# Reordering the start and the end of a fused convolution and maxout kernel: grouped transposes, one more column group with four taps on TensorE, relus ahead of copies, and a free bank and a merged store at the end

## The chip, the cores and the metric

The kernel runs on one core of a Trainium2 chip. A core has five engines with a queue of instructions each: TensorE (PE in the profile; its weight loads are shown apart as PEld), VectorE (DVE), ScalarE (ACT), GpSimd (POOL) and SyncE (SP, which here only issues DMAs). An engine works through its own queue in order; semaphores tie the queues together. The metric is the device time of one execution in microseconds (us). The kernel before takes 424.26 us, the median of 13 runs that lie between 422.1 and 426.3.

## The reference: what is computed

A dynamic convolution is followed by a maxout block. `x` is 8 x 4160 x 192; there are 8 heads of 24 channels, and every row and head has its own 7 weights.

```
w   = softmax(weight_gen, over the 7 taps)            # per row and head
y   = sum over k of w[.., k] * x_padded[row + k]       # causal: 6 zero rows ahead of each batch item
h1  = y @ w1 ; h2 = y @ w2                             # 33280 x 192 @ 192 x 1024
out = max(h1, h2) @ w_out                              # 33280 x 1024 @ 1024 x 192, float32
```

The kernel uses max(h1, h2) = h1 + relu(h2 - h1). So it computes relu(y @ (w2 - w1)) @ w_out + y @ (w1 @ w_out): one wide product in place of two, and a small one with the constant 192 x 192 matrix w1 @ w_out.

## The kernel before, in words

**Columns, batches, units, tiles, groups.** Partition p holds the rows 260p to 260p + 259. A *column* is one row of each partition: 128 rows. The 260 columns are taken in 17 *batches* of 16 (the last has 4). A batch is cut into *units*: four of 4 columns in batches 0 and 1, two of 8 columns afterwards, one of 4 at the end. A unit has as many *tiles* as columns; a tile is a [128 x 1024] block of hidden values in PSUM, which one or two of the eight 128-wide pieces of d_ff fill for all columns of the unit. Tiles are processed in *groups* (`GROUPS`, line 70): eight groups of two, then groups of three; the last group, with tile 259, has a single one. While a group's hidden tiles are made, the results of earlier columns (`OUTS`, line 366) are made too, two or four columns at a time. Eight columns are left when the groups are through; `rest_of_results` (line 426) makes them in three parts of 4, 2 and 2.

**The stages.** For each batch ACT takes exp of the weights (`exp_sum`, L127), DVE sums them over the taps (`red`, L132), ACT takes the log of the sum (`ln`, L135), DVE subtracts it (`shift`, L140), and ACT takes exp again, to bf16 (`weights`, L148). DVE multiplies seven shifted views of `x` by these (`mul`, L157, into `m_t`). The seven taps are then added and the result is transposed, in one of three ways:

- units 8 and up: DVE adds all (`adds`, L172, L177, L179, into `y_t`), a DMA issued on SP transposes (`transpose`, L188), and POOL waits for it with a small copy before it starts the next loads (L194);
- units 4 to 7: DVE makes the first add only (`adds(.., True)`, L172: taps 3 to 5 onto 0 to 2). TensorE multiplies the four taps left by the identity and accumulates them in PSUM, which transposes and adds at once (`sum_transpose`, L215), and ACT copies the sum out (L220);
- units 0 to 3: the same with all seven taps on TensorE.

`hid_tile` (L247) makes a hidden tile from the transposed `yt`, `relu` (L257, on ACT) moves it to `rd_t` in bf16. `out_first` (L299 and L287) and `out_second` (L287) accumulate results in a bank `op_ps`; half of the contributions use partitions 0 to 63 and half 64 to 127, and the second half waits, by an empty instruction on ACT (`relay`, L320), until the first is through. `evac` (L343) copies a result to `o_t`, and stores go out when a unit is complete (L353). The last two columns go apart (L333): one is copied on ACT and stored from ACT's queue, the other is copied on DVE and stored from SP's.

**Order.** The schedule is manual: each engine's instructions stand in the order in which the functions are called. The start (from line 450 on) is written out call by call. `early` (line 630) says what is put between the halves of groups 3 to 7, and `extra` (line 638) hangs the DVE, ACT and DMA work of later batches on tile numbers. Ahead of the work proper, TensorE multiplies the identity 115 times (`keep_warm`).

**PSUM.** In the start two pools of two buffers each are used: `h` for hidden tiles and `o` for everything else, in turn (column sums, the transposed w1 `tp`, the product `pw`, results). From group 8 on there are `ab` (2048 wide, the first two tiles of a group), `c` (1024, its last tile) and `r` (1024, the results), with one buffer each. A new tile in a pool waits for the last reader of the buffer that it takes over.

**w1 @ w_out.** `w1_transposed` (line 536) transposes the eight 128-wide pieces of w1 on TensorE: for each piece a part of 128 rows (`E`) and one of 64 (`T`), L542. Two ACT copies bring them to `w1t` (L548). `w10_product` (line 582) multiplies (L587), and five ACT copies (L595) write `w10`, which `out_first` needs.

Of the kernel before, what the change touches and what calls it, by code (L numbers as in the profile page):

```python
# [17 lines left out]
def _sub(base: bass.AP, off: int, dims):  # L18
    ap = [list(base.ap[0])] + [[int(s), int(c)] for s, c in dims]
    return dataclasses.replace(base, offset=base.offset + off, ap=ap)  # L20
# [3 lines left out]
def kernel(  # L24
# [9 lines left out]
    nc = tc.nc  # L34
# [90 lines left out]
    def exp_sum(b):  # L125
        e_ts[b] = pe_.tile([P, BATCHES[b][1] * WGC], FP32, name="e_t", tag="e")
        nc.scalar.activation(out=e_ts[b], in_=wg_ts[b], func=AF.Exp)  # L127

    def red(b):
        TH = BATCHES[b][1] * H  # L130
        s_ts[b] = psm.tile([P, TH], FP32, name="sum_t", tag="sum")
        nc.vector.reduce_sum(out=s_ts[b], in_=_sub(e_ts.pop(b), 0, [[K, TH], [1, K]]), axis=AX.X)  # L132

    def ln(b):
        nc.scalar.activation(out=s_ts[b], in_=s_ts[b], func=AF.Ln)  # L135
# [7 lines left out]
    def weights(b, o):  # L143

        N = dict(pieces(b))[o] * H
        if b not in en_ts:
            en_ts[b] = pen.tile([P, 16 * WGC * 2], BF16, name="en_t", tag="en")
        nc.scalar.activation(  # L148
            out=_sub(en_ts[b], o * WGC * 2, [[2 * N, K], [2, N], [1, 2]]),
            in_=_sub(wg_ts[b], o * WGC, [[1, K], [K, N], [0, 2]]), func=AF.Exp,  # L150
        )


    def mul(b, o):

        n = dict(pieces(b))[o]
        nc.vector.tensor_tensor(  # L157
            out=m_t[:, K * o * D:K * (o + n) * D],
            in0=_sub(xb_ts[b], o * D, [[D, K], [1, n * D]]),
            in1=_sub(en_ts[b], o * WGC * 2, [[2, K * n * H], [0, G // 2], [1, 2]]),  # L160
            op=ALU.mult,
        )
# [40 lines left out]
    def half(j):  # L203
        return slice(64 * j, 64 * j + 64)

    def sum_transpose(u, taps=range(K)):

        b, o, n = UNITS[u]
        nb = n // 2 * 3
        yps = ps["r" if "r" in ps else "o"].tile([P, 1024], FP32, name="yps", tag="op")  # L210
        for k in range(nb):
            for t in taps:
                for j in range(2):
                    at = (K * o + t * n + k // 3 + j * n // 2) * D + k % 3 * 64
                    nc.tensor.matmul(  # L215
                        yps[half(j), k * P:(k + 1) * P], lhsT=m_t[:, at:at + 64],
                        rhs=ident, start=(t == taps[0]), stop=(t == taps[-1]), skip_group_check=True,
                    )
        yt = pyt.tile([P, 8 // 2 * 3 * P], BF16, name="yt", tag="yt")
        nc.scalar.copy(out=yt[:, 0:nb * P], in_=yps[:, 0:nb * P])  # L220
        yt_ts[u] = yt
# [46 lines left out]
    def place(p):  # L268

        u, i, _ = column(2 * p)  # L270
        b, o, n = UNITS[u]
        return BATCHES[b][0] + o + i, n // 2
# [36 lines left out]
    def out_second(now, go):  # L309

        for c in now[::2]:
            for f in range(FCH):
                for j in range(2):
                    mm = out_hidden(c + 1 - j, f, j)
                    if c == now[0] and f == 0:
                        tc.add_manual_dep(mm.ins, go.ins.name, SYNC, reason="bank of the other half")
# [8 lines left out]
    def evac(p, n):  # L325

        tile_, at = op_at[p]
        o = o_t[0]
        if p == NT // 2 - 1:

            for j, copy, eng in ((0, nc.scalar.copy, nc.scalar), (1, nc.vector.tensor_copy, nc.sync)):
                c = place(p)[0] + 2 * j
                copy(out=o[:, c % 24 * D:(c % 24 + 1) * D], in_=tile_[:, at + j * 512:at + j * 512 + D])  # L333
                eng.dma_start(
                    out=bass.AP(tensor=out.tensor, offset=c * D, ap=[[CPP * D, P], [1, D]]),
                    in_=o[:, c % 24 * D:(c % 24 + 1) * D],
                )
            return
        runs = [[q for q in range(p, p + n) if column(2 * q)[0] == u]
                for u in range(column(2 * p)[0], column(2 * (p + n - 1))[0] + 1)]  # L340
        for qs in runs:
            c, h = place(qs[0])
            nc.scalar.copy(out=_sub(o, c % 24 * D, [[D, len(qs)], [h * D, 2], [1, D]]),  # L343
                           in_=_sub(tile_, at + (qs[0] - p) * D, [[D, len(qs)], [512, 2], [1, D]]))
        stores = []
        for q in range(p, p + n):
            u, i, _ = column(2 * q)
            if u < NU - 1 and i == UNITS[u][2] // 2 - 1:
                stores.append((place(q)[0] - i, 2 * (i + 1)))
            if u == NU - 1:  # L350
                stores.extend((place(q)[0] + 2 * j, 1) for j in range(2))
        for c, w in stores:
            nc.scalar.dma_start(  # L353
                out=bass.AP(tensor=out.tensor, offset=c * D, ap=[[CPP * D, P], [1, w * D]]),
                in_=o_t[0][:, c % 24 * D:(c % 24 + w) * D],
            )


# [32 lines left out]
    def out_room(now, tag=None):  # L391
        tag = tag or ("r" if "r" in ps else "o")
        w, name = {"ab": (2048, "ab"), "c": (1024, "c")}.get(tag, (1024, "op"))
        tile_ = ps[tag].tile([P, w], FP32, name="op_ps", tag=name)
        for c in now:
            op_at[c // 2] = tile_, (c - now[0]) // 2 * D

    def hidden(g, now=(), between=lambda: None, beside=lambda: None):


        t0, n = GROUPS[g]
        rd = room(g)
        for t in range(t0, t0 + n - 1):
            hid_tile(t)
        if now:
            out_room(now)
            last = out_first(now)
        if len(now) > 2:
            relu(rd, t0, n - 1)
        else:  # L410
            for t in range(t0, t0 + n - 1):
                relu(rd, t, 1)
        if now:
            go = relay(last)
        hid_tile(t0 + n - 1)
        if len(now) > 2:
            beside()
        relu(rd, t0 + n - 1, 1)
        between()
        if now:  # L420
            out_second(now, go)
            evac(now[0] // 2, len(now) // 2)
        if len(now) <= 2:
            beside()
# [25 lines left out]
    with tc.tile_pool(name="pstage", bufs=1) as pstage:  # L450
# [85 lines left out]
        def w1_transposed():  # L536

            tp = ps["o"].tile([P, 1024], FP32, name="tp", tag="op")[:, :].bitcast(BF16)
            for fi in range(FCH):
                o = fi // 4 * 1024 + fi % 4 * D  # L540
                for at, kind, nr in ((0, "E", P), (P, "T", 64)):
                    nc.tensor.matmul(  # L542
                        tp[:, o + at:o + at + nr],
                        lhsT=w1[kind][0:nr, fi * P:(fi + 1) * P],
                        rhs=ident[0:nr, 0:nr], is_transpose=True, skip_group_check=True,
                    )
            for h in range(2):
                nc.scalar.copy(out=w1t[:, 4 * h * D:4 * (h + 1) * D],  # L548
                               in_=tp[:, h * 1024:h * 1024 + 4 * D])

        warm = ps["h"].tile([P, 1024], FP32, name="warm", tag="hd")

# [15 lines left out]
        nc.scalar.copy(out=w1["T"], in_=ws["T", 0])  # L568
        w_diff(1, nc.vector.tensor_copy)
        mul(0, 8)  # L570
        sum_transpose(1)
        exp_sum(1)
        red(1)
# [1 line left out]
        ln(1)  # L575
        shift(1)
        mul(0, 12)
        w1_transposed()
        weights(1, 0)
        weights(1, 4)  # L580

        def w10_product():

# [13 lines left out]


        hidden(2)
        mul(1, 0)  # L600
        adds(1, 0, True)
        exp_sum(2)
        sum_transpose(2)
        load_x(2, 0, 16)
        load_wg(4, nc.gpsimd)
        red(2)
        mul(1, 4)
        adds(1, 4, True)
        hidden(3)
        w10_product()  # L610
        sum_transpose(3)
        weights(1, 8)
        weights(1, 12)
        ln(2)

    pout = ctx.enter_context(tc.tile_pool(name="pout", bufs=1))
    o_t.append(pout.tile([P, 24 * D], FP32, name="o_t", tag="o"))
# [2 lines left out]
    def rest_of_1():  # L620
        mul(1, 8)
        shift(2)
        adds(1, 8, True)
        mul(1, 12)
        red(3)
        adds(1, 12, True)


    none = lambda: None
    early = {  # L630
        3: (none, lambda: (exp_sum(3), rest_of_1())),
        4: (lambda: sum_transpose(4, (0, 1, 2, K - 1)), lambda: weights(2, 0)),
        5: (lambda: sum_transpose(5, (0, 1, 2, K - 1)), none),
        6: (lambda: (weights(2, 8), ln(3), sum_transpose(6, (0, 1, 2, K - 1))), lambda: load_x(3, 0, 8)),
        7: (lambda: sum_transpose(7, (0, 1, 2, K - 1)), none),
    }

    def extra(t):
# [29 lines left out]
    out_room(OUTS[3])  # L668
    go = relay(out_first(OUTS[3]))
    out_second(OUTS[3], go)  # L670
    evac(OUTS[3][0] // 2, len(OUTS[3]) // 2)
    early[3][1]()
    for g in range(4, len(GROUPS)):
# [40 lines left out]
```

## Time and profile before

| what | value |
|---|---|
| median of 13 runs | 424.26 us (422.1 to 426.3) |
| the profiled execution | 425.85 us, of which the span of the profile is 424.0 |
| TensorE clock granted, mean | 0.997 of full speed |
| ACT relus, L257, 128x1024 and 128x2048 | 206 instructions, 234.6 us |
| TensorE results, L287 | 4160 matmuls, 210.7 us |
| TensorE hidden tiles, L247 | 1584 matmuls, 187.4 us |
| DVE products, L157 | 37 instructions, 187.5 us |
| TensorE column sums, L215 | 528 matmuls, 16.5 us |
| instruction queue | 58 packets, 0.95 MB |

A timeline row gives the start in us from the start of the span, the time it covers in us, the engine, the line, the operation, what is written and read, the shapes, the number of instructions, and in square brackets the idle time before it with what ended it. "issue" there stands for nothing that the profile shows. Matmuls are pipelined and their ends are modelled, so the busy time of PE is no measure of its peak. The chain that ended last is followed back from the last instruction, at each step to what released it or to the instruction ahead of it on its engine.

### The profile page before, as it was taken

The page shows a single profiled execution, that of the slowest core. Times are in us where ns is not written, and L with a number is a line of the kernel's source. Part 1 is how long each engine was busy: PE and PEld are TensorE (multiplying, and loading weights), DVE is VectorE, ACT ScalarE, POOL GpSimd, SP SyncE. Part 2 cuts the span into 40 slices and gives each one's busy share as a digit, 9 for nine tenths or more (in the row PEclk, how much of TensorE's full clock was granted, in tenths as well). Part 3 has the DMA queues.
Part 4 walks back from the last instruction along what each step waited for, and adds up shares of the span by engine and source line. Part 5 has one row for each costly group of instructions (what it writes and reads, how often), then busy time and mean ns, then how long its engine had stood idle before and what let it go on. Part 6 is the DMA issues. An engine that isn't in the chain of part 4 may idle for free.

```text
span 424.0 us, 15949 instructions
## 1 busy us (share of the span) xinstructions
PE 406.7 (96%) x7405; PEld 329.3 (78%) x7405; DVE 377.1 (89%) x176; ACT 360.2 (85%) x416; POOL 69.9 (16%) x102
## 2 busy tenths in 40 slices
PE   7988999999999999999999999999999999999984
PEld 7867899877778777877777777877777777777784
DVE  5989998998999999999999999999999999996000
ACT  5795979999998989898989999898999899787851
POOL 1510102221112221222111212201311121210000
PEclk9999999999999999999999999999999999999998
DMA  8975436577687677965867677687796586556213
GB/s 249 255 160 147 112 77 157 99 161 125 170 193 154 183 174 100 237 166 125 233 112 176 169 177 191 146 147 197 98 251 165 89 211 116 117 157 129 80 77 114
DMA packets 60259, 65.70 MB, mean 155 GB/s; under 512 B 47617, under 2 KB 48513, under 8 KB 60192
## 3 DMA queue, kind: packets, MB, share of 16 engines
q0 software_dynamic: 8128, 24.11, 28.4%
q1 hardware_dynamic: 46448, 15.10, 21.7%
q10 hardware_dynamic: 5616, 25.46, 15.5%
q8 instruction: 58, 0.95, 0.9%
q14 instruction: 9, 0.07, 0.1%
HBM read 35.96 MB, written 25.56 MB: 145 GB/s over the span
## 4 chain that ended last, share of the span: by engine, by line
DVE 57%; PE 31%; ACT 7%; issue 4%; ACTq 1%; POOL 0%; DVEq 0%; POOLq 0%
DVE m_t L157 28%; DVE m_t L172 12%; PE op_ps L287 11%; DVE m_t L177 9%; PE hd L247 8%; ACT rd_t L257 4%; PE yps L215 4%; PE hdp L247 3%; DVE y_t L179 3%; DVE wg_t L140 3%; DVE sum_t L132 2%; PE warm L556 2%; PE op_ps L299 2%; ACT o_t L343 1%; ACTq L353 1%
## 5 line engine op out<-in xcount | busy, mean ns | idle before, releaser
L257 ACT ACTIVATE rd_t<-hd 128x1024 bf16<-128x1024 f32 (+1 forms) x206 | 234.6, 1183 | 31.4 <-PE hd L247 31.0
L287 PE MATMUL op_ps<-wo,rd_t 64*128 64x192 bf16 x4160 | 210.7, 243 | 1.9 <-issue 1.8
L287 PEld LDWEIGHTS <-rd_t 64*128 64x128 bf16 x4160 | 180.2, 94 | 18.2 <-issue 2.1
L247 PE MATMUL hd<-yt,wd 64*128 64x512 bf16 (+1 forms) x1584 | 187.4, 360 | 0.9 <-ACT rd_t L257 0.9
L157 DVE TENSOR_TENSOR m_t<-xb_t,en_t 128x10752 bf16<-128x10752 bf16 (+1 forms) x37 | 187.5, 5070 | 0.5 <-ACT rd_t L257 0.3
L247 PEld LDWEIGHTS <-wd 64*128 64x128 bf16 x1776 | 93.1, 94 | 43.4 <-issue 3.6
L194 POOL CAST gate<-yt 128x1 f32<-128x1 bf16 x29 | 34.0, 1172 | 285.9 <-DMA yt<-y_t 285.9
L172 DVE TENSOR_TENSOR m_t<-m_t 128x4608 bf16<-128x4608 bf16 (+1 forms) x33 | 78.2, 2368 | 0.1
L343 ACT COPY o_t<-op_ps 128x384 f32<-128x384 f32 (+1 forms) x99 | 56.9, 586 | 12.5 <-PE op_ps L287 12.4
L299 PE MATMUL op_ps<-w,yt 64*128 64x192 bf16 x780 | 55.4, 243 | 4.4 <-ACT o_t L343 4.4
L299 PEld LDWEIGHTS <-yt 64*128 64x128 bf16 x780 | 38.7, 94 | 21.4 <-issue 6.6
L177 DVE TENSOR_TENSOR m_t<-m_t 128x3072 bf16<-128x3072 bf16 (+1 forms) x29 | 50.2, 1730 | 1.0
L148 ACT ACTIVATE en_t<-wg_t 128x896 bf16<-128x896 f32 (+1 forms) x37 | 34.1, 935 | 1.9 <-ACT o_t L343 1.2
L333 DVE COPY o_t<-op_ps 128x192 f32<-128x192 f32 x1 | 0.4, 358 | 31.4 <-ACT o_t L333 31.4
L179 DVE TENSOR_TENSOR y_t<-m_t 128x1536 bf16<-128x1536 bf16 (+1 forms) x29 | 27.4, 944 | 1.0
L132 DVE TENSOR_REDUCE sum_t<-e_t 128x128 f32<-128x896 f32 (+1 forms) x17 | 17.7, 1038 | 5.3 <-ACT e_t L127 5.3
L115 POOL DMA_DIRECT2D xb_t<-in_x_dram x32 | 17.3, 540 | 23.8 <-DVE m_t L157 23.1
L140 DVE TENSOR_TENSOR wg_t<-wg_t,sum_t 128x896 f32<-128x896 f32 (+1 forms) x17 | 17.8, 1045 | 3.0 <-ACT sum_t L135 3.0
L127 ACT ACTIVATE e_t<-wg_t 128x896 f32<-128x896 f32 (+1 forms) x17 | 15.8, 930 | 3.9 <-DMA wg_t<-in_weight_gen_dram 3.0
L257 ACT ACTIVATE rd_t<-hdp 128x1024 bf16<-128x1024 f32 x16 | 15.7, 1027 | 1.9 <-PE hdp L247 1.8
L215 PE MATMUL yps<-ident,m_t 128*64 128x128 bf16 x528 | 16.5, 220 | 0.0
L215 PEld LDWEIGHTS <-m_t 128*64 128x64 bf16 x528 | 15.2, 110 | 1.4 <-issue 1.3
(45 smaller groups left out, 89.6 us busy)
## 6 DMA issues: line engine op xcount, KB each, us to landing
out_dram<-o_t ACTq DMA_DIRECT2D x28, 768.0 KB, 4.6
xb_t<-in_x_dram POOLq DMA_DIRECT2D x28, 384.0 KB, 5.1
wg_t<-in_weight_gen_dram POOLq DMA_DIRECT2D x14, 448.0 KB, 6.2
xb_t<-xb_t POOLq DMA_DIRECT2D x16, 288.0 KB, 5.5
out_dram<-o_t ACTq DMA_DIRECT2D x8, 384.0 KB, 4.5
wg_t<-in_weight_gen_dram SPq DMA_DIRECT2D x2, 448.0 KB, 5.5
xs<-in_x_dram SPq DMA_DIRECT2D x2, 384.0 KB, 6.6
xb_t<-in_x_dram POOLq DMA_DIRECT2D x1, 768.0 KB, 8.0
```

Source lines behind the costliest of these rows:

```text
L148: nc.scalar.activation(out=_sub(en_ts[b], o * WGC * 2, [[2 * N, K], [2, N], [1, 2]]), in_=_sub(wg_ts[b], o * WGC, [[1, K], [K, N], [0, 2]] ...
L157: nc.vector.tensor_tensor(out=m_t[:, K * o * D:K * (o + n) * D], in0=_sub(xb_ts[b], o * D, [[D, K], [1, n * D]]), in1=_sub(en_ts[b], o * W ...
L172: nc.vector.tensor_tensor(out=taps(0, 1, 3), in0=taps(0, 1, 3), in1=taps(3, 1, 3), op=ALU.add)
L177: nc.vector.tensor_tensor(out=taps(0, 2, 2), in0=taps(0, 2, 2), in1=taps(1, 5, 2), op=ALU.add)
L179: nc.vector.tensor_tensor(out=_sub(y_ts[b], o * D, [[64, 2], [P, 3 * w // 2], [1, 64]]), in0=taps(0, 1, 1), in1=taps(2, 1, 1), op=ALU.add,)
L194: nc.gpsimd.tensor_copy(out=gate, in_=yt[:, 0:1])
L215: nc.tensor.matmul(yps[half(j), k * P:(k + 1) * P], lhsT=m_t[:, at:at + 64], rhs=ident, start=(t == taps[0]), stop=(t == taps[-1]), skip_g ...
L247: nc.tensor.matmul(hid_out(t, f, j), lhsT=wd[half(j), s * F + f * P:s * F + (f + 1) * P], rhs=_sub(yt_ts[u][half(j), :], (s + j) % 3 * P, ...
L257: nc.scalar.activation(out=rd[:, k * 1024:(k + n) * 1024], in_=hd[:, at:at + n * 1024], func=AF.Relu)
L287: return nc.tensor.matmul(op_out(c), lhsT=rd[half(r), k * 1024 + at:k * 1024 + at + P], rhs=wo[half(r), f * D:(f + 1) * D], start=False, s ...
L299: nc.tensor.matmul(op_out(c + j), lhsT=yt_ts[u][half(j), (3 * i + (s + j) % 3) * P:(3 * i + (s + j) % 3 + 1) * P], rhs=w10[half(j), s * D: ...
L343: nc.scalar.copy(out=_sub(o, c % 24 * D, [[D, len(qs)], [h * D, 2], [1, D]]), in_=_sub(tile_, at + (qs[0] - p) * D, [[D, len(qs)], [512, 2 ...
```

## The change

1. `w1_transposed` makes the eight transposes with 128 rows first and then the eight with 64. It returns the PSUM tile, and the two copies to `w1t` move behind the call `hidden(2)`, as do `weights(1, 0)` and `weights(1, 4)`. On ACT the two relus of group 2 now stand ahead of them.
2. Unit 2 (columns 8 to 11) gets the first add on DVE (`adds(0, 8, True)`, ahead of the sum for batch 1) and only four taps on TensorE (`LEFT`).
3. `exp_sum(2)` and `red(2)` move behind `w10_product`, `adds(1, 4, True)` with them; `ln(2)` moves behind the second halves of the first results, ahead of their copy-out. `exp_sum(3)`, `red(3)` and `adds(1, 12, True)` move behind group 4, so its relus stand ahead of that exp.
4. The results that are made in the last group, which has one tile, go to bank `ab` instead of `r`.
5. In the last unit, the two columns of a pair that `evac` copies together are stored by one DMA on SP's queue, where there were two on ACT's.

```diff
+    LEFT = (0, 1, 2, K - 1)
...
             if u < NU - 1 and i == UNITS[u][2] // 2 - 1:
-                stores.append((place(q)[0] - i, 2 * (i + 1)))
+                stores.append((nc.scalar, place(q)[0] - i, [1, 2 * (i + 1) * D]))
             if u == NU - 1:
-                stores.extend((place(q)[0] + 2 * j, 1) for j in range(2))
-        for c, w in stores:
-            nc.scalar.dma_start(
-                out=bass.AP(tensor=out.tensor, offset=c * D, ap=[[CPP * D, P], [1, w * D]]),
-                in_=o_t[0][:, c % 24 * D:(c % 24 + w) * D],
+                stores.append((nc.sync, place(q)[0], [2 * D, 2], [1, D]))
+        for eng, c, *ap in stores:
+            eng.dma_start(
+                out=bass.AP(tensor=out.tensor, offset=c * D, ap=[[CPP * D, P], *ap]),
+                in_=_sub(o_t[0], c % 24 * D, ap),
             )
...
         if now:
-            out_room(now)
+            out_room(now, "ab" if n == 1 and "ab" in ps else None)
             last = out_first(now)
...
-            for fi in range(FCH):
-                o = fi // 4 * 1024 + fi % 4 * D
-                for at, kind, nr in ((0, "E", P), (P, "T", 64)):
+            for at, kind, nr in ((0, "E", P), (P, "T", 64)):
+                for fi in range(FCH):
+                    o = fi // 4 * 1024 + fi % 4 * D
                     nc.tensor.matmul(
...
-            for h in range(2):
-                nc.scalar.copy(out=w1t[:, 4 * h * D:4 * (h + 1) * D],
-                               in_=tp[:, h * 1024:h * 1024 + 4 * D])
+            return tp
...
         mul(0, 8)
+        adds(0, 8, True)
         sum_transpose(1)
...
-        w1_transposed()
-        weights(1, 0)
-        weights(1, 4)
+        tp = w1_transposed()
...
         hidden(2)
+        for h in range(2):
+            nc.scalar.copy(out=w1t[:, 4 * h * D:4 * (h + 1) * D], in_=tp[:, h * 1024:h * 1024 + 4 * D])
+        weights(1, 0)
+        weights(1, 4)
         mul(1, 0)
         adds(1, 0, True)
-        exp_sum(2)
-        sum_transpose(2)
+        sum_transpose(2, LEFT)
         load_x(2, 0, 16)
         load_wg(4, nc.gpsimd)
-        red(2)
         mul(1, 4)
-        adds(1, 4, True)
         hidden(3)
         w10_product()
+        exp_sum(2)
+        red(2)
+        adds(1, 4, True)
         sum_transpose(3)
         weights(1, 8)
         weights(1, 12)
-        ln(2)
...
         mul(1, 12)
+
+    def end_of_1():
+        exp_sum(3)
         red(3)
         adds(1, 12, True)
...
-        3: (none, lambda: (exp_sum(3), rest_of_1())),
-        4: (lambda: sum_transpose(4, (0, 1, 2, K - 1)), lambda: weights(2, 0)),
+        3: (none, rest_of_1),
+        4: (lambda: sum_transpose(4, LEFT), lambda: (end_of_1(), weights(2, 0))),
...
     out_second(OUTS[3], go)
+    ln(2)
     evac(OUTS[3][0] // 2, len(OUTS[3]) // 2)
```

The profiled program has 36 matmuls fewer, one DVE instruction more, one DMA less on ACT's queue and one more on SP's.

More of the change, by code (lines that the diff above doesn't have):

```diff
@@ L630 @@
     early = {
-        3: (none, lambda: (exp_sum(3), rest_of_1())),
-        4: (lambda: sum_transpose(4, (0, 1, 2, K - 1)), lambda: weights(2, 0)),
-        5: (lambda: sum_transpose(5, (0, 1, 2, K - 1)), none),
-        6: (lambda: (weights(2, 8), ln(3), sum_transpose(6, (0, 1, 2, K - 1))), lambda: load_x(3, 0, 8)),
-        7: (lambda: sum_transpose(7, (0, 1, 2, K - 1)), none),
+        3: (none, rest_of_1),
+        4: (lambda: sum_transpose(4, LEFT), lambda: (end_of_1(), weights(2, 0))),
+        5: (lambda: sum_transpose(5, LEFT), none),
+        6: (lambda: (weights(2, 8), ln(3), sum_transpose(6, LEFT)), lambda: load_x(3, 0, 8)),
+        7: (lambda: sum_transpose(7, LEFT), none),
     }
```

## The prediction

> **What bounds the kernel now.** I read the chain that ended last first, then the idle rows of each engine in time order, because the chain's shares alone mislead here.
>
> ```profile
> PE 406.7 (96%) x7405; PEld 329.3 (78%) x7405; DVE 377.1 (89%) x176; ACT 360.2 (85%) x416; POOL 69.9 (16%) x102
> DVE 57%; PE 31%; ACT 7%; issue 4%; ACTq 1%; POOL 0%; DVEq 0%; POOLq 0%
> ```
>
> VectorE (DVE) holds 57% of the chain, but DVE is free from 389.05 us on and TensorE (PE) works to 418.64. So I ask who waits in between. From 37 to 408 us the PE timeline has ten gaps, none over 0.5 us, and none of them ends on a transposed y. DVE has two real gaps, both on ScalarE (ACT), which itself follows PE:
>
> ```profile
> 67.50 1.09 DVE L132 TENSOR_REDUCE sum_t<-e_t 128x128 f32<-128x896 f32 x1 [1.87 <-ACT e_t L127]
> 105.00 1.09 DVE L140 TENSOR_TENSOR wg_t<-wg_t,sum_t 128x896 f32<-128x896 f32 x1 [1.65 <-ACT sum_t L135]
> ```
>
> After 105 DVE never waits: 11.92 us for eight columns (adds at 106.00 and 117.92), against 11.45 on PE (twelve hidden tiles take from 373.48 to 390.65, 17.17 us). So PE slowly closes in on DVE, and is closest near 367 us:
>
> ```profile
> 367.34 2.08 POOL L194 CAST gate<-yt 128x1 f32<-128x1 bf16 x1 [11.43 <-DMA yt<-y_t]
> 368.40 1.47 PE L247 MATMUL hd<-yt,wd 64*128 64x512 bf16 x12
> ```
>
> That y landed at 367.34 and PE wants it at 368.40: 1.06 us to spare. PE's order sets the end, with DVE just behind it. A gain on PE in the first 60 us therefore reaches the end only if DVE comes forward too. Its two gaps (1.87 + 1.65 = 3.52 us) give it that room, as both end on ACT steps that move with PE.
>
> In the start, PE itself stands still for nothing that the profile shows:
>
> ```profile
> 27.91 0.72 PE L247 MATMUL hdp<-yt,wd 64*128 64x256 bf16 x10
> 29.69 0.94 PE L247 MATMUL hdp<-yt,wd 64*128 64x256 bf16 x14 [1.07 <-issue]
> ...
> 34.71 0.49 PE L287 MATMUL op_ps<-wo,rd_t 64*128 64x192 bf16 x8
> 36.71 0.51 PE L287 MATMUL op_ps<-wo,rd_t 64*128 64x192 bf16 x8 [1.50 <-issue]
> ```
>
> Counting matmuls from the start (115 warm, 84, 14, 24, and so on), these gaps stand before matmuls 479 and 607, and smaller ones before 223 (16.75), 351 (22.67) and 991 (53.04): always a multiple of 128 apart. 128 matmuls with their weight loads are 256 instructions, and the instruction queue moves such blocks (58 packets, 0.95 MB, 16 KB each). I read them as late instruction blocks. While the first loads run, one block comes per 5.9 to 7.0 us (16.75, 22.67, 29.69, 36.71).
>
> The end, last:
>
> ```profile
> 408.98 0.42 PE L299 MATMUL op_ps<-w,yt 64*128 64x192 bf16 x6 [0.95 <-ACT o_t L343]
> ...
> 412.19 0.42 PE L299 MATMUL op_ps<-w,yt 64*128 64x192 bf16 x6 [0.82 <-ACT o_t L343]
> ```
>
> ```profile
> 418.53 1.48 ACTq L353 DMA_DIRECT2D out_dram<-o_t  x2
> 420.05 0.32 ACT L333 COPY o_t<-op_ps 128x192 f32<-128x192 f32 x1 [1.55 <-issue]
> ```
>
> PE twice waits for the one result bank to be copied out. Then ACT issues two stores (1.48 us) while the last result has been ready since 418.64 (matmuls at 416.48, 2.16 long).
>
> **The last results.** The last group has one tile, so its big bank `ab` is free: its relu (404.27, 1.88 long) ends at 406.15, before PE's 408.03. Both waits go: 0.95 + 0.82 = 1.77 us. What comes next is not late: the first part of the rest needs bank `r`, copied by 408.92 and wanted at about 410.3; the second needs `ab` again, copied about 411.2 and wanted after 412.
>
> **One store for two.** The two small stores leave ACT's queue. ACT's last copy can start at about 418.69 in the old time instead of 420.05: 1.36 us. The DVE copy (0.08 us after ACT's) and the last store follow it. SyncE (SP) has had nothing since its transposes near 390, so the merged store waits for nobody; the last store stands behind it, but 0.9 us later, and an issue took 0.34 to 0.97 us in these rows. Together 3.13 us, if the transfers allow it. They may not: a store of 768 KB runs until about 420.0, then four of 96 KB. If these cannot overlap the big one and go at the 209 GB/s of this window, they need 1.9 us after 418.2, and end at 420.1 against 422.2: only 2.1 us.
>
> ```profile
> DMA  0010000000299951000000000001898966461000
> GB/s 0 0 33 0 0 0 0 0 0 0 123 442 406 406 197 33 0 0 0 0 0 0 0 0 16 0 0 33 356 393 369 393 209 221 164 215 39 0 0 0
> ```
>
> Slices are 0.5 us from 404. In the last five the engines are only 10 to 60% busy, so the small stores were paced by their issue; I take 2.8, nearer 3.13.
>
> **Four taps for columns 8 to 11, DVE's side.** One more add of 2304 elements, 1.36 us (five such rows, mean 1355 ns). It starts at 21.34, where DVE idled 0.57 for ACT's exp; the sum then ends at about 23.7 instead of 22.96. The log waits on ACT behind two relus ending 23.68, so it comes 0.2 late, and DVE with it. DVE's 0.94 wait there is used up. From then on DVE is 0.2 later (product of columns 8 to 11 of the next batch at 37.5 instead of 37.30); the moved sums and adds are the same count. The Pool (POOL) loads that follow the product of columns 12 to 15 start at 28.6 instead of 28.40; DVE first reads what they bring at 47.95. It costs nothing at the end: the two gaps hold 3.52. Without these it would cost 0.2, or at worst 1.36.
>
> **PE's side.** 36 of 84 matmuls go from that column sum: 84 take 2.47 us in the chain (2.54 with the drain), so 36 are 1.06 us.
>
> **w1's transposes.** Sixteen, alternating 128 and 64 rows, take 2.5 us (21.50 to 24.00) with a 0.22 us block gap, 0.14 us each. Fourteen plain 128x128 matmuls took 0.89, 0.064 each. Grouped they would save up to 1.25, at least 0; I take 0.9. The next hidden tiles need relus that end at 23.68, so some 0.2 of it waits there.
>
> **First relus ahead of copies, and the moved exp, sum and log.** By ACT's own rows, in the new order: log to 24.1; two relus (1.95) to 26.0; two copies of w1 (1.50) to 27.5; two weights (1.15) to 28.5; the copy of column sums (0.83) to 29.2; two relus to 31.1; five copies of the product (1.51) to 32.5; exp (0.98), a copy (0.80) and two weights (1.11) to 35.0; then the relay. The log that stood ahead of the relay now stands behind it, and waits for DVE's sum at 36.3: covered, as the copy-out behind it needs PE until 36.8 at the earliest. The exp for batch 3, now behind the next group's copy-out (44.48 before, about 1.5 earlier now), is done near 44.5, and DVE wants it at 45.5. The weights that DVE needs at 28.04 are ready at 27.9. By this chain PE's second halves of the first results start at 35.1 instead of 38.22: 3.1 us earlier. That is the upper bound.
>
> **The blocks.** Block 351 comes as before, at 22.67. If the next two again take 7.0 us, 479 and 607 cannot run before 29.69 and 36.71. With 36 matmuls fewer, 479 is the seventh of the column sum that PE reaches at 29.4, and 607 the seventh of the second halves. From 36.71 there remain 26 of these 32 at 0.047 us, 1.2, to 37.9, where before this step ended at 39.48: 1.55 us. So the wait taken away on ACT is replaced by PE's own instruction stream, and the transposes' 0.9 is swallowed by it. The lower bound is -0.1: the block after these, for 735, came within 5.8 us before; wanted at about 42.1 and 7.0 us after 36.71 it would come at 43.7 and take 1.6 back. I take 1.5, near the value by this case's own rows. The Trainium skill ("Runtime: NRT & Kernel Launch", section "Instruction fetch mechanics") calls the price of crossing a 16 KiB block mostly hidden; the 1.07 and 1.50 us gaps here disagree. By that rule the sum would take 3.1 in place of 1.5, and the time would be 418.4.
>
> **Sum.** 1.5 + 2.8 = 4.3 us. The profiled execution took 425.85 (span 424.0, 1.85 around it), which gives 421.55. It lies 1.59 above the median of the thirteen runs, 424.26; against that the forecast is 420.0.
>
> **The rivals.** *The blocks don't bind:* early 3.1, end 2.8, 418.4. For it: blocks from 607 on came in 5.8 us or less. Against: the same loads run to 36 us. *Nothing early:* the 0.2 us on DVE and a late block eat it; only the end counts, 424.26 - 2.8 = 421.5. *Late y:* DVE does not come forward, and PE runs into the y of 367 us; early gain limited to 1.06, 424.26 - 3.9 = 420.4. Against it: DVE's gaps end on ACT. *The bank is not free after all*, so that the end gives only 1.36 and the start 1.5: 421.4. *Slower:* later instruction blocks. Moved by 36, the next four (735, 863, 991, 1119) fall behind other transfers and each stalls as 607 did, 1.50: 6.0 lost, 4.3 gained, 426.0. It decides from the third such stall on (4.5). Against: before, only one of these four stalled, by 0.31.
>
> **How the numbers follow.** Forecast 48%, blocks don't bind 18%, late y 6%, nothing early 12%, bank 7%, slower 9%. The first two and the late y all lie over 0.3% (1.27 us, about what runs of this kernel can tell from none) below 424.26, as do nothing early and bank if their end is right; a share of these two (6 points) I leave within 0.3%, for an end that the transfers hold back. So faster 0.85, same 0.06, slower 0.09. The likeliest case alone spans 419.0 to 421.3 (end 2.1 to 3.13, early 0.9 to 2.2). The range runs from 417.9 (3.1 + 3.13 with a little for run to run) to 422.4 (early -0.1, end 2.1, and run to run).
>
> **What would show it.** Right: the idle rows of 0.95 and 0.82 us gone; ACT's last copy within 0.1 us of PE's end; block gaps before matmuls 479 and 607 still near 29.7 and 36.7, the first halves waiting for the five copies at 32.5; DVE's gaps at 67 and 105 shorter, its adds after 105 about 1.5 earlier. Wrong: PE idle on a y, DVE gaps unchanged, new issue gaps after 40 us, or a last transfer that ends as late after PE as before.

## The result, and the profile after

The changed kernel takes 418.83 us, the median of 11 runs (418.44 to 424.02); the kernel before stands at 424.15 over 48 runs. The ratio is 0.9896, with a 95% interval of 0.9873 to 0.992: 3.4 to 5.4 us less. By the medians it is 5.3 us, by the middle of that interval 4.4. The forecast was 420.0, in a range from 417.9 to 422.4.

The profiled execution took 418.79 us (span 417.0) where that of before took 425.85 (span 424.0). These two differ by 7.06 us, more than the medians, and the experiments show why: the execution shown of the kernel before was an unlucky one in its start.

The page of the changed kernel, its busy times and the shares of the chain that ended last:

```profile
PE 403.9 (97%) x7369; PEld 327.3 (78%) x7369; DVE 378.0 (91%) x177; ACT 359.9 (86%) x416; POOL 68.6 (16%) x102
PE 49%; DVE 28%; ACT 15%; issue 4%; DMA 2%; SPq 1%; ACTq 0%; DVEq 0%
```

PE has 36 matmuls less and DVE one instruction more. Two stores of 96 KB are gone from ACT's queue (the text on the change says one), and SP's queue has one of 192 KB more. The chain's shares have changed sides, DVE from 57% to 28%, although DVE does more work than before: where two engines keep pace, this view says little on which of them must become faster.

The start, PE's timeline in the changed kernel:

```profile
22.68 0.27 PE L545 MATMUL tp<-ident,w1E 128*128 128x128 bf16 x2 [0.66 <-issue]
...
32.31 0.42 PE L302 MATMUL op_ps<-w,yt 64*128 64x192 bf16 x6 [0.70 <-ACT w L595]
...
35.74 0.82 PE L250 MATMUL hdp<-yt,wd 64*128 64x256 bf16 x12
```

After 22.68 no gap in the start ends on "issue". The two gaps of 1.07 and 1.50 us are gone; the only wait left there is 0.70 us for the five copies of the product. Group 4 starts at 35.74 instead of 39.56, and group 8 at 53.74 instead of 57.83, 4.09 us earlier.

DVE follows, in its timeline:

```profile
65.24 1.08 DVE L132 TENSOR_REDUCE sum_t<-e_t 128x128 f32<-128x896 f32 x1
...
100.99 1.08 DVE L140 TENSOR_TENSOR wg_t<-wg_t,sum_t 128x896 f32<-128x896 f32 x1
102.00 2.55 DVE L172 TENSOR_TENSOR m_t<-m_t 128x4608 bf16<-128x4608 bf16 x1
```

Both of its gaps (1.87 and 1.65 us) are gone; the add that stood at 106.00 stands at 102.00. So the y that was tightest, from POOL's and PE's timelines, is still there in time, with 0.63 us to spare instead of 1.06:

```profile
363.77 1.65 POOL L194 CAST gate<-yt 128x1 f32<-128x1 bf16 x1 [11.86 <-DMA yt<-y_t]
```

```profile
364.40 1.48 PE L250 MATMUL hd<-yt,wd 64*128 64x512 bf16 x12
```

The end, the timeline of all engines:

```profile
403.85 0.43 PE L302 MATMUL op_ps<-w,yt 64*128 64x192 bf16 x6
...
406.07 0.43 PE L302 MATMUL op_ps<-w,yt 64*128 64x192 bf16 x6
...
410.36 2.16 PE L290 MATMUL op_ps<-wo,rd_t 64*128 64x192 bf16 x48
...
412.40 0.41 SPq L356 DMA_DIRECT2D out_dram<-o_t  x1
412.56 0.32 ACT L336 COPY o_t<-op_ps 128x192 f32<-128x192 f32 x1 [0.18 <-PE op_ps L290]
...
413.35 0.34 SPq L337 DMA_DIRECT2D out_dram<-o_t  x1
```

Both waits for bank `r` are gone. Ahead of them PE is 4.00 us earlier than before (398.75 against 402.75), after the first 5.13 (403.85 against 408.98), after the second 6.12 (406.07 against 412.19). ACT's last copy starts 0.04 us after PE's end (412.52) and so 7.49 earlier; the last store is issued 7.49 earlier. The span is only 7.0 shorter: 0.5 us go back in the transfers, which now follow each other without a gap (slices of 0.5 us from 404):

```profile
GB/s 0 0 123 430 418 406 197 33 0 0 0 0 16 0 0 0 467 406 381 333 333 314 126 0 0 0 0 0 0 0 0 0 0 0 0 0 0 0 0 0
```

One thing in the end has nothing to do with the stores. The instruction queue moved 58 packets of 16 KB before and moves 57 now, since the program has 36 matmuls fewer. The 58th ran from 417.70 to 418.62, just when the last store of 768 KB began to move. The DMA view of the kernel before from 417.5 us on shows that packet, and how many us that store took to land:

```profile
q8 instruction: 1, 0.02, 1.2%
...
out_dram<-o_t ACTq DMA_DIRECT2D x1, 768.0 KB, 4.4
```

In the same view of the changed kernel from 404 us on, the two stores of this size took 3.3:

```profile
out_dram<-o_t ACTq DMA_DIRECT2D x2, 768.0 KB, 3.3
```

By the packets in the trace, 123 of the store's 128 large ones had ended by 420.21 before, and the other five ended one by one, 0.23 us apart, up to 421.23. In the changed kernel all 128 had ended by 414.11. From PE's end to the end of the last transfer it was 3.67 us and is now 2.78. The experiments show how much of this belongs to the packet.

### The profile page after: what moved, and what is told of

Read it like the earlier page. It is cut to its first block, busy times and chain, and to the rows that moved or that the text cites. A ratio compares the mean times of both kernels' runs of the same rounds, so it can differ in the third digit from the quotient of the medians.

```text
span 417.0 us, 15881 instructions
## 1 busy us (share of the span) xinstructions
PE 403.9 (97%) x7369; PEld 327.3 (78%) x7369; DVE 378.0 (91%) x177; ACT 359.9 (86%) x416; POOL 68.6 (16%) x102
## 3 DMA queue, kind: packets, MB, share of 16 engines
q0 software_dynamic: 8128, 24.11, 28.3%
## 4 chain that ended last, share of the span: by engine, by line
PE 49%; DVE 28%; ACT 15%; issue 4%; DMA 2%; SPq 1%; ACTq 0%; DVEq 0%
PE op_ps L290 23%; PE hd L250 20%; DVE m_t L157 15%; ACT rd_t L260 9%; DVE m_t L172 5%; PE op_ps L302 4%; DVE m_t L177 4%; ACT en_t L148 2%; DMA ws1T<-in_moe_w_dram 2%; ACT o_t L346 1%; DVE sum_t L132 1%; DVE y_t L179 1%; DVE wg_t L140 1%; PE hdp L250 1%; PE yps L218 1%
## 5 line engine op out<-in xcount | busy, mean ns | idle before, releaser
L172 DVE TENSOR_TENSOR m_t<-m_t 128x4608 bf16<-128x4608 bf16 (+1 forms) x34 | 79.5, 2338 | 0.1
L194 POOL CAST gate<-yt 128x1 f32<-128x1 bf16 x29 | 32.8, 1130 | 280.7 <-DMA yt<-y_t 280.7
L218 PE MATMUL yps<-ident,m_t 128*64 128x128 bf16 x492 | 15.3, 220 | 0.1
L218 PEld LDWEIGHTS <-m_t 128*64 128x64 bf16 x492 | 14.1, 110 | 1.6 <-issue 1.5
```

What stands on the lines that cost most here:

```text
L172: nc.vector.tensor_tensor(out=taps(0, 1, 3), in0=taps(0, 1, 3), in1=taps(3, 1, 3), op=ALU.add)
L194: nc.gpsimd.tensor_copy(out=gate, in_=yt[:, 0:1])
L218: nc.tensor.matmul(yps[half(j), k * P:(k + 1) * P], lhsT=m_t[:, at:at + 64], rhs=ident, start=(t == taps[0]), stop=(t == taps[-1]), skip_g ...
```

## The experiments

Times are medians, in us; each comparison is with the kernel before on the same chip. For the start there is a second measure from the profiles: the time from the first column sum on PE to the first hidden tiles of group 8. In the profiled executions of before and after it is 45.60 (12.23 to 57.83) and 41.40 (12.34 to 53.74).

**The start alone.** The changed kernel with its end undone:

```diff
-            out_room(now, "ab" if n == 1 and "ab" in ps else None)
+            out_room(now)
...
-                stores.append((nc.sync, place(q)[0], [2 * D, 2], [1, D]))
+                stores.extend((place(q)[0] + 2 * j, 1) for j in range(2))
```

> All edits to the start, none to the end (results of the last group again in bank r, two stores on ACT's queue). If the start is worth what the two profiled executions show (TensorE 4.0 us earlier at the hidden tiles that begin at 57.8 us), the median falls by 3.5 to 4.5 us against the kernel before. If the execution shown of the kernel before was an unlucky one (it took 425.85, 1.6 over its median), by 2 to 3 us. By the prediction's step, 1.5 us. TensorE's two waits near the end, 0.95 and 0.82 us, are back in any case.

420.94 against 424.01, ratio 0.9943 (0.9913 to 0.9973): 3.1 us by the medians, 1.1 to 3.7 by the interval. The start took 41.17. The median lies just above the second of the three cases, twice the prediction's step; the interval leaves all three open. Not all of it is the start. The profiled execution has 57 packets of instructions, and although it still has the two small stores, its last transfer ends 3.03 us after PE's end, 0.64 sooner than before.

**The end alone, and the bank alone.** The kernel before with both edits to the end, and with the bank only:

```diff
-            out_room(now)
+            out_room(now, "ab" if n == 1 and "ab" in ps else None)
```

> The kernel before with the two edits to the end alone. From the profiles the bank is worth 2.1 us on TensorE (1.77 by its idle rows) and the freed ACT queue 1.4 us, of which the transfers take back 0.5: 3.0 us less than the kernel before. If the transfers hold the end instead, 2.1 us or less.

> The kernel before with the last group's results in bank ab, the two stores still on ACT's queue. 2.1 us less than the kernel before, if the start gain and the end add up; ACT's last copy still 1.4 us after TensorE's end. If the stores' transfers set the end, under 1 us.

Both edits: 422.63 against 424.01, ratio 0.9946 (0.9912 to 0.998). The bank alone: 421.26, ratio 0.9933 (0.99 to 0.9965). The intervals cover each other, so these runs don't show what the merged store adds. The fastest runs are 419.99 and 419.87, where the kernel before has 421.68: some 1.7 to 1.8 us for the end either way, less than the 3.0 expected for both edits. With the bank alone the wait on ACT is there as expected:

```profile
413.71 1.57 ACTq L353 DMA_DIRECT2D out_dram<-o_t  x2
415.32 0.32 ACT L333 COPY o_t<-op_ps 128x192 f32<-128x192 f32 x1 [1.64 <-issue]
```

but taking it away helps only as far as the transfers allow, and these depend on the 58th packet. From PE's end to the last transfer's end it is 3.62 to 3.76 us in the four executions with two small stores and 58 packets, and 3.03 in the one with 57. With the merged store it is 3.59, 3.67 and 4.14 in the three with 58, and 2.77 to 2.78 in the four with 57. In all seven with 58 the last large store takes 4.3 to 4.8 us to land, in the five with 57 it takes 3.3. So a packet less is worth 0.6 to 0.7 us of the end with two small stores and 0.8 to 1.4 with the merged one. The merged store itself gains 0.25 with 57 packets (3.03 to 2.78) and nothing that shows with 58. The profiled execution with both edits also met a late y, the rival that PE runs into DVE's chain, once in its course:

```profile
298.32 2.60 PE L247 MATMUL hd<-yt,wd 64*128 64x512 bf16 x12 [2.77 <-DMA yt<-y_t]
```

**The kernel before, again.**

> The kernel before once more, for a second profile. If the gaps before matmuls 479 and 607 come from the instruction blocks' place in time against the loads, they are there again within some tenths of a us or change between executions; if something in the program sets them, both are 1.07 and 1.50 us again.

421.47, and PE's timeline has neither gap:

```profile
26.65 1.63 PE L247 MATMUL hdp<-yt,wd 64*128 64x256 bf16 x24
...
32.39 0.84 PE L287 MATMUL op_ps<-wo,rd_t 64*128 64x192 bf16 x16
```

The 24 hidden matmuls of group 3 and the first results run through. So the program alone does not set these gaps; they differ from execution to execution. The start took 41.83 here, 43.12 and 42.79 in the two runs with an edited end (with one gap of 0.34 us, and with 0.28 and 0.49), 45.60 in the execution that the prediction was made from. With the changed start it was 41.17, 41.40, 42.35, 41.62 and 41.13. At its luckiest the old start takes as long as the changed one does; on average of these few it is 1.8 us slower.

**Seven taps.**

```diff
-        adds(0, 8, True)
...
-        sum_transpose(2, LEFT)
+        sum_transpose(2)
```

> The changed kernel with seven taps again for columns 8 to 11: 36 matmuls more on TensorE, one add less on VectorE. Theory 1, the start now follows ACT's order and TensorE has 0.7 us to spare before the five copies of the product: 0.4 to 1.0 us slower than the changed kernel (418.8), so 419.2 to 419.8. Theory 2, the change helped because it moved the limits of the instruction blocks by 36 matmuls: block gaps before matmuls 479 and 607 return in many executions, and it is 2 us or more slower, 421 or above.

422.35, against 418.83 and 419.24 for the changed kernel and 419.06 for the next run, on the same chip: at least 3 us slower, as theory 2 has it. (To the kernel before the ratio is 0.9961, 0.9932 to 0.9989.) Its profiled execution, which took 424.44 and so is one of the slower ones, has both gaps back, at the same matmuls 479 and 607 and within 0.4 us of the same places as in the kernel before:

```profile
27.00 0.72 PE L250 MATMUL hdp<-yt,wd 64*128 64x256 bf16 x10
29.70 0.94 PE L250 MATMUL hdp<-yt,wd 64*128 64x256 bf16 x14 [1.98 <-issue]
...
34.72 0.49 PE L290 MATMUL op_ps<-wo,rd_t 64*128 64x192 bf16 x8
37.09 0.50 PE L290 MATMUL op_ps<-wo,rd_t 64*128 64x192 bf16 x8 [1.89 <-issue]
```

PE reaches the first limit 1 us earlier than before (27.72 against 28.63) and waits 0.9 longer for it. In this execution all that ACT's new order had won is swallowed, as the prediction feared for the whole change. The program is also back at 58 packets, and its last transfer ends 4.14 us after PE's end instead of 2.78.

**Copies first.** The changed kernel with ACT's old order at that place:

```diff
         tp = w1_transposed()
+        for h in range(2):
+            nc.scalar.copy(out=w1t[:, 4 * h * D:4 * (h + 1) * D], in_=tp[:, h * 1024:h * 1024 + 4 * D])
+        weights(1, 0)
+        weights(1, 4)
```

> The changed kernel with the two copies of w1 and the two weights ahead of group 2's relus again. Theory 1: the relus come up to 2.65 us later, TensorE waits for their buffers at group 3, and the first results follow 1 to 2.5 us later: 420 to 421.3. Theory 2: the blocks stand where they stood in the changed kernel, so within 0.5 us of it, 418.8.

419.06. PE waits 1.57 us for the relus at group 3, as theory 1 says:

```profile
26.90 1.75 PE L250 MATMUL hdp<-yt,wd 64*128 64x256 bf16 x24 [1.57 <-ACT rd_t L260]
```

and then doesn't wait for the product's copies. Its start took 42.36, as long as the slowest of the changed ones (41.13 to 42.35). By the medians no loss can be told from the noise, by the one profile it is up to 1 us. The moved exp, sum and log were not undone, so what they are worth was not tested.

**Alternating transposes.**

```diff
-            for at, kind, nr in ((0, "E", P), (P, "T", 64)):
-                for fi in range(FCH):
-                    o = fi // 4 * 1024 + fi % 4 * D
+            for fi in range(FCH):
+                o = fi // 4 * 1024 + fi % 4 * D
+                for at, kind, nr in ((0, "E", P), (P, "T", 64)):
```

> The changed kernel with w1's transposes alternating again. They take about 2.3 us instead of about 0.9 (both without the block gap). If TensorE's 0.7 us of waiting before the first results and the relus cover it, the time stays within 0.5 us of 418.8; if it is on the path, 0.7 us or more slower.

419.78, ratio 0.99 (0.9847 to 0.9953), the runs from 418.29 to 421.69 and one of 424.71: unclear between the two cases. The sixteen transposes took 2.7 us (20.29 to 23.00, a block gap of 0.42 in it), against 1.6 grouped (21.51 to 23.13, a gap of 0.66 in it).

**The blocks moved back.**

```diff
-        keep_warm(115)
+        for _ in range(72):
+            nc.tensor.matmul(warm[:, 0:64], lhsT=ident, rhs=ident[:, 0:64],
+                             start=True, stop=True, skip_group_check=True)
+        keep_warm(79)
```

> The changed kernel with 36 of the first 115 warming matmuls each cut into two of half the width: the same streaming time, 36 matmuls more, so that the limits of the instruction blocks stand again where they stood in the kernel before (matmul 443 of the old count is now 479). Theory 2: gaps without a releaser return before matmuls 479 or 607, and the median rises by 1 to 3 us. Theory 1: no change within 0.5 us of 418.8.

420.08, about 1 us slower, but not by these two gaps. They don't return. The gap one block earlier, before matmul 351, is 1.00 us instead of 0.66, and the 36 extra matmuls have moved it from the transposes into the second column sum:

```profile
17.81 1.34 PE L218 MATMUL yps<-ident,m_t 128*64 128x128 bf16 x42
20.15 0.36 PE L218 MATMUL yps<-ident,m_t 128*64 128x128 bf16 x6 [1.00 <-issue]
```

But its start took 42.24, no longer than others of the changed start. Of the 1.30 us by which its span exceeds that of the changed kernel, 0.89 lie behind PE's end (3.67 against 2.78): the program has 58 packets again. So 36 matmuls more in the warm-up, far from the stores, cost in this profile most of what they cost at the end. That moving the limits brings the two gaps back, as theory 2 had it, is not confirmed.

**Later loads.** The kernel before, with the loads for batch 2 held back:

```diff
+        nc.gpsimd.tensor_copy(out=gate, in_=m_t[:, 0:1])
         load_x(2, 0, 16)
```

> The kernel before, with a small GpSimd copy that waits for the add of batch 1's first columns put ahead of the loads that follow the product of columns 12 to 15; these loads start at about 33 us instead of 28.4. If the block for matmul 607 is late because its fetch stands behind these loads, the gap of 1.50 us before 607 goes, that before 479 (behind the loads issued from 19 to 21 us) stays, and the median falls by 0.5 to 1.5 us against the kernel before. If the blocks are late whatever the loads do, no change.

423.17 against 423.68, ratio 0.9992 (0.9968 to 1.0015): no change. In its profiled execution the first of these loads is issued at 32.79, the gap before 607 is gone, and 0.24 us is left of that before 479:

```profile
28.61 0.94 PE L247 MATMUL hdp<-yt,wd 64*128 64x256 bf16 x14 [0.24 <-issue]
```

One execution without a gap proves little, since the unchanged kernel has such executions too, and the median moves by 0.5 us, not to be told from none. That holding back these loads helps is not shown.

**The packets in the traces.** The kept traces hold each packet of the instruction queue with its time. In the fourteen executions PE's timeline has 25 gaps of 0.2 us or more at the limits from 223 to 991. After each of them PE goes on 1.2 to 1.6 us after the end of a packet; at limits without such a gap the packet had ended 1.2 to 4.8 us before. So these gaps are late instruction blocks, as the prediction read them. The next packet starts at about the time PE goes over a limit (0.3 us ahead at the earliest) or later, and how much later differs: 2.4 to 4.7 us at 223 and 351, while GpSimd's first loads run in all executions. At 863 it is 3.05 and 3.25 us in the two executions in which PE comes there after the loads of about 47 us have begun, and at most 0.4 in the twelve others. At 479 the loads for batch 2 begin at about the same moment, and it is anything from none to 5.0 us. This speaks for the loads as what delays the packets. One execution of the changed kernel speaks against it, with 4.0 us at 479 although its loads began 0.6 us later, so it stays a likely cause, not a shown one.

The traces also show what four taps do. From the limit 351 to the limit 479, the wait for the block left out, PE takes 5.0 us with seven taps and 5.8 to 6.0 in the old start. In the changed kernel it takes 6.6 to 7.2, as 36 later and mostly longer matmuls have moved into this block. So the packet has more time to come.

**The changed kernel again, and a better one.** The second execution of the changed kernel, and the changed kernel with the last full unit stored in two halves:

```diff
+            if u == NU - 2:
+                if i % 2:
+                    stores.append((nc.scalar, place(q)[0] - 1, [4 * D, 2], [1, 2 * D]))
-            if u < NU - 1 and i == UNITS[u][2] // 2 - 1:
+            elif u < NU - 1 and i == UNITS[u][2] // 2 - 1:
```

> The changed kernel once more, for a second profile and for comparison with the next two on the same chip: 418.5 to 419.5 us, hidden tiles of group 8 again between 53.4 and 53.8 us, or up to 1.5 later where a block is late.

> The changed kernel, with the last unit of eight columns stored in two halves, the first some 4 us earlier. If the transfers hold the end (the last one ends 1.95 us after its issue, where it was 1.47 before), 0.3 to 0.5 us less than the changed kernel; if the issue of the last store sets it, no change.

> As the run with the split store, and the weights of batch 3 are loaded behind the product of columns 12 to 15 instead of at 21 us. If the loads issued from 19 to 21 us hold back the block for matmul 479, its fetch comes earlier than 26 us and the slow executions of the changed kernel (420 and more) get rarer: median 0 to 0.5 us below that of the split store. If more loads at 28 us hold back the block for 607 instead, 0.5 to 2 us slower.

The changed kernel: 419.24. Its second execution has a gap before 607 after all:

```profile
34.95 1.25 PE L290 MATMUL op_ps<-wo,rd_t 64*128 64x192 bf16 x26 [0.83 <-issue]
```

The split store: 418.02. The run meant to load less early took 417.82, but its edit left the order of POOL's queue as it was (the wait stands on the load behind the one that was moved), so it is the split store a second time and tells nothing on the loads. Both medians are below the changed kernel's on the same chip, by 1.2 and 1.4 us, but with six runs each the intervals to the kernel before cover each other (0.986 to 0.9923 for the changed kernel, 0.9845 to 0.9936 and 0.9835 to 0.9902). The part that the profiles explain is 0.6: from PE's end to the last transfer's end it is 2.18 us in both, where the changed kernel has 2.78 and 2.77. The first half is out before the last stretch, which now carries less:

```profile
GB/s 0 0 160 406 418 393 197 54 350 341 66 25 0 0 0 0 313 381 188 320 321 51 0 0 0 0 0 0 0 0 0 0 0 0 0 0 0 0 0 0
```

This version has the lowest median here: ratio 0.9868 (0.9835 to 0.9902) to the kernel before in its second run.

## Why the prediction was right or wrong

**The bound.** Right. PE's order sets the end, and DVE came forward with it: its gaps at 67 and 105 us took up the 4 us, and no y was late in the profiled execution. That DVE is close behind is shown by the late y of 2.77 us in one run, a rival given 6 in 100.

**DVE's extra add.** Right: the subtraction starts at 24.11 instead of 23.91, 0.2 us later as worked out; the add hides in the two waits.

**The transposes.** They took 2.28 us without the gap and now take 0.96. That saves 1.32, a little more than the 1.25 that was the most expected (0.9 was taken). It is not clearly on the path.

**ACT's order.** The chain worked out for ACT gave 35.1 us for the second halves of the first results; they started at about 34.4, since the relay (34.34) doesn't wait for the end of the exp ahead of it (34.82) and most steps overlap by 0.1. But putting the copies ahead of the relus again costs nothing that the medians show, while seven taps cost 3 us, 1.4 of them behind PE's end in the profiled execution. Of the parts that were undone, the four taps are the one that the gain needs.

**The blocks.** This is the step that failed. It held that blocks 479 and 607 cannot come before 29.69 and 36.71, and so priced the start at 1.5. In the changed kernel they come in time in one execution, and in another the second is 0.83 late. That the gaps are late blocks was right; but the gap lengths of a single execution were taken for the blocks' own pace, while the old start shows executions with both gaps, with one and with none. By the medians the start alone is worth 3.1 us, of which about 0.6 belongs to the missing 58th packet at the end; by the profiles the start is worth 1.8 on average. The interval of the runs, 1.1 to 3.7, holds the 1.5 too, so it is the reasoning that is refuted, and not the size. The fastest runs are 421.59 to 421.77 us with the kernel before and 418.17 and 418.44 with the changed one, some 3.3 less. The other 2 us of the medians' 5.3 come from executions well above the fastest, which have become rarer. That late blocks make these slower executions fits the profiles, but most of these runs were not profiled. The rival "the blocks don't bind", given 18 in 100, describes the profiled execution, and its 418.4 is nearer to 418.83 than the forecast. The Trainium skill's sentence that such crossings are mostly hidden ("Runtime: NRT & Kernel Launch", "Instruction fetch mechanics") would also have led there, though the gaps of 1.98 and 1.89 us with seven taps show that "mostly" can fail for 3.9 us in one execution.

**The bank.** The mechanism was right. PE won 2.12 us there and not 1.77, as the idle rows count from the modelled end of the matmul before, and in the changed kernel the next starts 0.18 before such an end (403.85, against 402.53 + 1.50).

**The store.** This term was too large. ACT's copy came forward as worked out, 1.37 us with the last store behind it (7.49 against 6.12), and of the forecast's 2.8 for the end 1.03 stood for that. But the last transfer comes only 0.89 us closer to PE's end, and 0.64 of it is there with the two small stores too, by the missing packet. The store's own part is about 0.25. The prediction saw that the transfers might not allow the gain, but let the large store run until about 420.0; its last packets ended at 421.23, behind a packet of instructions that it didn't count. The end is worth 1.7 to 2.1 us by the fastest runs and on top of the start (420.94 to 418.83, on two chips), near the 2.1 that the prediction gave for transfers that hold the end.

So the two terms missed in opposite directions, by the medians the start by +1.6 and the end by -0.7, and the sum, 4.3, lies 1.0 under the 5.3 of the medians and beside the 4.4 of the ratio. That it came so near is in part luck: the start was reasoned from gaps that an execution may or may not have, and a packet of instructions at the end stood in neither term.

## What to carry to other kernels

A gap that ends on nothing, at every 128th matmul, was the instruction stream here: look for a packet of the instruction queue just before its end, and before pricing it from one profile, take a second, because its length can be chance. 36 matmuls fewer ahead of such limits were worth some 3 us here, at the loads and at the end together, three times the 1.06 estimated for their duration. And in the last microseconds look at the transfers too: here a wait of 1.37 us taken off an engine paid about 0.25, while one instruction block less during the last large store paid 0.6 to 1.4.

## What the runs showed of the hardware

- The 128-row and the 64-row transposes of w1 take 0.14 us each on average when they alternate (2.28 us for sixteen), and 0.06 when grouped (0.96 us for sixteen), block gaps left out.
- Of two stores issued back to back on ACT's queue behind one of 768 KB, the pair took 1.44 to 1.57 us in the four executions with the 58th packet of instructions, and 1.00 in the one without; a single store takes 0.34 in the changed kernel.
- The same program's start varied from 41.83 to 45.60 us, by gaps at the limits of 256 instructions. PE goes on 1.2 to 1.6 us after the end of the packet that it waited for. What makes a block late in one execution and not in the next is likely GpSimd's loads, but holding back those of batch 2 did not clearly change the median.
- A 16 KB packet of instructions (0.9 to 1.3 us) that ran just as a store of 768 KB began made that store land after 4.3 to 4.8 us instead of 3.3.
